# One attention and GLU decode step on one core: output weights loaded in sixteen pieces of eight partitions

## The chip, the cores and the metric

The kernel runs on one core of one Trainium2 chip. Time is device microseconds (us) of one execution, given as the median of several runs. The core has the engines TensorE (PE in the profile), VectorE (DVE), ScalarE (ACT), GpSimd (POOL) and SyncE (SP), and 16 DMA engines that move data between the chip's memory (HBM) and the on-chip memory (SBUF, 128 partitions). In this kernel SP issues every transfer, on one queue that each of the 16 DMA engines serves in order.

## The reference

The step takes `x` of 4 sequences, one token each, D = 512, and computes, in bf16:

```
h   = x + Attention(LayerNorm(x))
out = h + GLU(LayerNorm(h))

q = LN(x) @ wq                     # 32 heads of 128
p = softmax(q k^T / sqrt(128))     # k_cache, v_cache: [4, 32, 8192, 128]
Attention = (p v) @ wo             # wo: [4096, 512]
GLU = (sigmoid(LN(h) @ w_gate) * (LN(h) @ w_up)) @ w_down    # F = 1792
```

The two caches hold 128 pairs of sequence and head, and each pair has 2 MB of K and 2 MB of V: 537 MB that are read once. All weights together are 13.9 MB, of which `wo` is 4.2 MB.

## The kernel before

**Heads.** The 128 pairs ("heads" from here on, `NH`) are worked off one after another. A K head is transposed on TensorE (`transposes`, L360), copied from PSUM to SBUF by ScalarE and VectorE in turn (L370, L372) and multiplied with the query (`scores`, L385). Eight heads make a group, whose softmax is done at once. Nine heads later (`LAGH`) the V head is multiplied with the probabilities (`pv`, L469; L481 in the last group). After each group, `finish` and `project` bring the eight results through the output weights (L498) and add them to the residual. At the end come the second LayerNorm and the GLU (L593, L609).

**The ring.** K and V heads, and at the end the three GLU weights, go through a ring of eight slots of 2 MB (`NSL`, `KV`). `take_slot` hands the slots out in turn, and a load into a slot waits until TensorE has finished with the head that held it.

**The order of the loads.** All loads stand in one list, `order`: K head n at place 4n, V head n at place 4(n + 9), so ten K heads come first and then V and K in turn. `wq` is put behind K head 0. `pump` walks the list in the order of the program and emits a load on SP's queue as soon as the program knows what it must wait for; the chip keeps that order. A load that waits holds up all loads behind it.

**Output weights.** `wo` (4096 x 512) lies in `Wreg` as 128 partitions of 32 heads of 512 values: row 128 h + p of `wo` goes to partition p, place h. `Wreg` holds `wq` first, so every `wo` load waits for the end of the q projection (`t_qproj`, L533). Before the change there are four loads (L302), one behind each of K heads 2, 3, 4 and 5. Load i brings heads 8i to 8i + 7 of all 128 partitions: 1,024 rows of 1 KB, 1 MB. Each load has a semaphore of its own, and `project` waits for all four before its first matmul.

Of the kernel before, what the change touches and what calls it, by code (L numbers as in the profile page):

```python
# [13 lines left out]
NKT = 16  # L14
LAGH = 9
GH = 8


class _Prog:
# [27 lines left out]
    def emit(self, eng, fn, waits=(), incs=1):  # L47

        todo = self._waits(eng, waits)
        tok = self.token(eng, incs) if incs else None  # L50

        def run(e):
            for key, v in todo:
                e.wait_ge(self.sems[key], v)
            made = fn(e)
            made = made if isinstance(made, list) else [made]
            if incs:
                assert len(made) == incs
                for m in made:
                    m.then_inc(self.sems[eng], 1)  # L60

        self.ops[eng].append(run)
        return tok
# [14 lines left out]
def bass_sequential_preLN__mha_block_cached__glu_gated_glu__decode_kernel(  # L78
# [20 lines left out]
    NH = B * H  # L99
    NG = NH // GH  # L100
    SCALE = float(DH) ** -0.5
# [3 lines left out]
    prog = _Prog()  # L105
    emit = prog.emit

    with ExitStack() as es:
        def SB(name, shape, dt):
            return es.enter_context(nc.sbuf_tensor(name, shape, dt))  # L110

        ident = SB("ident", [128, 128], BF16)
        identf = SB("identf", [128, 128], FP32)
        M8 = SB("M8", [128, GH], FP32)
        Gmat = SB("Gmat", [128, 128], FP32)
# [10 lines left out]
        q_all = SB("q_all", [128, NH], BF16)  # L126
        Lq = SB("Lq", [128, 2, GH * W], BF16)
        KV = SB("KV", [128, NSL, R * 128], BF16)
        kTc = SB("kTc", [128, NKT, 512], BF16)
        S_sb = SB("S_sb", [128, 512], FP32)  # L130
        E_sb = SB("E_sb", [128, 512], BF16)
        PT = SB("PT", [128, 2, NK * GH * 32], BF16)
        mpart = SB("mpart", [128, 1], FP32)
        mrow = SB("mrow", [1, GH], FP32)
        negmb = SB("negmb", [128, 1], FP32)
        sig = SB("sig", [128, 1], FP32)
        rsum = SB("rsum", [128, 1], FP32)
        O_sb = SB("O_sb", [128, 512], FP32)
        OT = SB("OT", [128, 2, GH], BF16)
        sg_sb = SB("sg_sb", [128, NFT * B], FP32)  # L140
# [7 lines left out]
        wo_v = Wreg[:, :].rearrange("p (h f) -> p h f", h=H)  # L148
# [15 lines left out]

        keys = ["sp", "act", "dve", "pool", "pe", "x", "out", "wg", "wu", "wd0", "wd1"]
        keys += [f"sl{i}" for i in range(NSL)] + [f"k0p{i}" for i in range(4)] + [f"vl{i}" for i in range(4)]
        keys += [f"wq{i}" for i in range(4)] + [f"wo{i}" for i in range(4)]
        for k in keys:
            prog.sems[k] = es.enter_context(nc.semaphore("s_" + k))

# [17 lines left out]
        def cols(t, c):  # L188
            return t[:, c:c + NDC * (B - 1) + 1:NDC]
# [107 lines left out]
        t_wo = []  # L297
        t_qproj = []

        def emit_wo(i):  # L300
            src = A_wo.rearrange("(h p) f -> p h f", p=128)
            t_wo.append(prog.dma("sp", f"wo{i}", lambda e: e.dma_start(  # L302
                wo_v[:, 8 * i:8 * (i + 1), :], src[:, 8 * i:8 * (i + 1), :]), [t_qproj[0]]))

        order = []
        for n in range(NH):
# [2 lines left out]
        order.sort()  # L309
        order = [(k, n) for _, _, k, n in order]  # L310
        order.insert(1, ("wq", 0))
        for i, after in enumerate((2, 3, 4, 5)):
            order.insert(order.index(("k", after)) + 1, ("wo", i))
        order.insert(order.index(("v", NH - 3)), ("wg", 0))
        order += [("wu", 0), ("wd", 0)]
        t_w = {}
# [7 lines left out]
        def pump():  # L324
            while next_dma[0] < len(order) and ready(*order[next_dma[0]]):
                kind, n = order[next_dma[0]]
                next_dma[0] += 1
                if kind == "k":
                    emit_head("k", n, k_src(n), t_k, "k0p" if n == 0 else "")
                elif kind == "v":  # L330
                    emit_head("v", n, v_src(n), t_v, "vl" if n == NH - 1 else "")
                elif kind == "wq":
                    emit_wq()
                elif kind == "wo":
                    emit_wo(n)
                else:
                    emit_weight(kind)
# [152 lines left out]
        def project(g, t_ot):  # L490
            ob = g % 2

            def f(e):
                ins = None
                for c in range(NDC):
                    for hh in range(2):
                        h = 2 * g + hh
                        ins = e.matmul(cols(bank[XO][:, 64:64 + NDC * B], c), wo_v[:, h, 128 * c:128 * (c + 1)],  # L498
                                       OT[:, ob, B * hh:B * (hh + 1)], start=(hh == 0), stop=(hh == 1))
                return ins  # L500
            t = emit("pe", f, [t_ot, *t_wo])
            st_["ot"][ob] = t
            st_["h"] = st_["xo"] = emit("dve", lambda e: e.tensor_tensor(
                sth[:, 0:NDC * B], sth[:, 0:NDC * B], bank[XO][:, 64:64 + NDC * B], ALU.add), [t, st_["h"]])

        def finish(g):
            ob = g % 2
            t_oev[g] = emit("act", lambda e: e.activation(O_sb[:, :], bank[OBK], ACT.Copy),  # L508
                            [t_pvg[g], st_.get("sel")])
            box = {}  # L510

            def s1():
                def f(e):
                    ins = None
                    for q in range(4):
                        ins = e.matmul(bank[XO][:, 0:GH], O_sb[:, 128 * q:128 * (q + 1)],  # L516
                                       selq[:, q:q + 29:4], start=(q == 0), stop=(q == 3))
                    return ins
                t = emit("pe", f, [t_oev[g], t_sel, st_["xo"]])
                st_["sel"] = t  # L520
                box["ot"] = emit("dve", lambda e: e.tensor_copy(OT[:, ob, :], bank[XO][:, 0:GH]),  # L521
                                 [t, st_["ot"][ob]])

            def s2():
                project(g, box["ot"])
            return [(4, s1), (6, s2)]
# [22 lines left out]
        for u in range(4 * (NH + LAGH)):  # L549
# [20 lines left out]
            if vu >= 0:  # L570
                pv(vu // 4, vu % 4)
                if vu % 32 == 31 and vu // 32 < NG - 1:
# [8 lines left out]
        t_ot = emit("dve", lambda e: e.tensor_copy(OT[:, gl % 2, :], bank[OBK][:, 0:GH]),  # L581
                    [t_pvg[gl], st_["ot"][gl % 2]])
        project(gl, t_ot)
        t_hn, _ = layernorm(sth, st_["h"], 1, hnT, bank[XS], st_["xs"])

# [91 lines left out]
```

## Time and profile before

| | |
|---|---|
| median of 3 runs | 1316.87 us (1316.83 to 1317.15) |
| span of the profiled execution, first to last instruction | 1315.5 us |
| TensorE busy | 1016.4 us, 77% |
| VectorE busy | 721.1 us, 55% |
| ScalarE busy | 608.7 us, 46% |
| SP's DMA queue, share of the 16 DMA engines' time | 99.0% |
| bytes moved | 552.68 MB, mean 420 GB/s |
| a `wo` load of 1 MB, issue to landing (median) | 14.1 us |
| first matmul of `project` (L498) | 159.7 us |

The span covers one execution under the hardware profiler. It is 1.4 us shorter than the median of the timed runs, which also holds what lies before the first and after the last instruction. The slices of the page cut the span into 40 equal parts; a digit is the busy share in tenths, and GB/s is what all 16 DMA engines moved together. In the table of waits, "A <- B: us, times, longest" says for how long A stood still until B was done. Rows of the windows give, for each stretch, the busy time of PE, PEld (weight loads), DVE, ACT and POOL with the number of instructions, then the granted TensorE clock, the DMA share and GB/s. The trace also keeps a record of every DMA packet with its start, duration and size, and of every time at which a DMA engine counted a transfer's semaphore up.

### The profile page before, as it was taken

The page shows a single profiled execution, that of the slowest core. Times are in us where ns is not written, and L with a number is a line of the kernel's source. Part 1 is how long each engine was busy: PE and PEld are TensorE (multiplying, and loading weights), DVE is VectorE, ACT ScalarE, POOL GpSimd, SP SyncE. Part 2 cuts the span into 40 slices and gives each one's busy share as a digit, 9 for nine tenths or more (in the row PEclk, how much of TensorE's full clock was granted, in tenths as well). Part 3 has the DMA queues.
Part 4 walks back from the last instruction along what each step waited for, and adds up shares of the span by engine and source line. Part 5 has one row for each costly group of instructions (what it writes and reads, how often), then busy time and mean ns, then how long its engine had stood idle before and what let it go on. Part 6 is the DMA issues. An engine that isn't in the chain of part 4 may idle for free.

```text
span 1315.5 us, 29564 instructions
## 1 busy us (share of the span) xinstructions
PE 1016.4 (77%) x13385; PEld 671.9 (51%) x13385; DVE 721.1 (55%) x1210; ACT 608.7 (46%) x1095; POOL 9.0 (1%) x11
## 2 busy tenths in 40 slices
PE   6887877877788787887788778788887878778764
PEld 5654544545455454554455445455554545545443
DVE  5774655556555565555556456555555656556520
ACT  3664544545444454444445445454444545445420
POOL 2000000000000000000000000000000000000000
PEclk8988888888888888788888888888788888888865
DMA  9999999999999999999999999999999999999996
GB/s 381 415 427 426 427 427 427 425 428 425 428 425 426 427 425 428 424 427 426 427 426 426 426 428 424 427 425 428 427 424 426 426 428 425 426 427 428 425 411 245
DMA packets 45510, 552.68 MB, mean 420 GB/s; under 512 B 4420, under 2 KB 10312, under 8 KB 12360
## 3 DMA queue, kind: packets, MB, share of 16 engines
q1 hardware_dynamic: 45384, 550.79, 99.0%
q8 instruction: 105, 1.72, 0.5%
q14 instruction: 21, 0.17, 0.0%
HBM read 550.77 MB, written 0.00 MB: 419 GB/s over the span
## 4 chain that ended last, share of the span: by engine, by line
DMA 81%; PE 16%; SPq 2%; ACT 0%; issue 0%; DVE 0%
DMA KV<-in_A_v_cache_dram 76%; PE PS L360 10%; PE PS L385 3%; PE PS L469 3%; DMA KV<-in_B_w_down_dram 2%; DMA KV<-in_A_k_cache_dram 1%; SPq L277 1%; DMA Wreg<-in_A_wq_dram 1%; SPq L302 0%; SPq L295 0%; ACT kTc L370 0%; SPq L274 0%; ACT L422 0%; PE PS L533 0%; PE PS L481 0%
## 5 line engine op out<-in xcount | busy, mean ns | idle before, releaser
L372 DVE CAST kTc<-PS 128x512 bf16<-128x512 f32 x1024 | 676.1, 692 | 484.4 <-PE PS L360 481.6
L370 ACT ACTIVATE kTc<-PS 128x512 bf16<-128x512 f32 x1024 | 573.4, 595 | 648.2 <-PE PS L360 646.2
L360 PEld LDWEIGHTS PS<-ident,KV 128*128 128x128 bf16 x8192 | 547.5, 109 | 252.3 <-ACT kTc L370 135.7
L360 PE MATMUL PS<-ident,KV 128*128 128x128 bf16 x8192 | 654.7, 240 | 12.8 <-DMA KV<-in_A_k_cache_dram 10.4
L469 PE MATMUL PS<-KV,PT 128*32 128x512 bf16 x1920 | 216.8, 442 | 242.2 <-DMA KV<-in_A_v_cache_dram 242.2
L385 PE MATMUL PS<-kTc,Lq 128*32 128x512 bf16 x2048 | 227.1, 435 | 1.1 <-DVE Lq L545 0.6
L469 PEld LDWEIGHTS PS<-KV,PT 128*32 128x32 bf16 x1920 | 52.4, 99 | 273.9 <-DMA KV<-in_A_v_cache_dram 273.6
L385 PEld LDWEIGHTS PS<-kTc,Lq 128*32 128x32 bf16 x2048 | 53.5, 95 | 64.6 <-issue 19.1
L481 PE MATMUL PS<-PT,KV 128*128 128x1 bf16 x512 | 14.9, 165 | 18.0 <-DMA KV<-in_A_v_cache_dram 15.4
L481 PEld LDWEIGHTS PS<-PT,KV 128*128 128x128 bf16 x512 | 14.3, 104 | 18.6 <-DMA KV<-in_A_v_cache_dram 15.9
L516 PE MATMUL PS<-selq,O_sb 128*128 128x8 f32 x120 | 16.7, 266 | 7.1 <-ACT O_sb L508 7.1
L516 PEld LDWEIGHTS PS<-selq,O_sb 128*128 128x128 f32 x120 | 15.3, 200 | 10.0 <-ACT O_sb L508 10.0
L409 DVE TENSOR_REDUCE mrow<-PS 1x8 f32<-1x128 f32 x16 | 4.5, 279 | 29.2 <-PE PS L405 29.2
L205 ACT ACTIVATE lnw<-lnw 128x4 f32<-128x4 f32 x2 | 0.4, 205 | 38.9 <-DVE lnw L202 38.9
L581 DVE CAST OT<-PS 128x8 bf16<-128x8 f32 x1 | 0.2, 167 | 32.6 <-PE PS L481 32.6
L521 DVE CAST OT<-PS 128x8 bf16<-128x8 f32 x15 | 2.5, 167 | 19.5 <-PE PS L516 19.5
L422 ACT ACTIVATE E_sb<-S_sb,negmb 128x512 bf16<-128x512 f32 x16 | 11.6, 722 | 3.1 <-DVE negmb L420 2.6
L400 DVE TENSOR_REDUCE mpart<-S_sb 128x1 f32<-128x512 f32 x16 | 11.0, 686 | 3.1 <-ACT S_sb L398 1.5
L508 ACT ACTIVATE O_sb<-PS 128x512 f32<-128x512 f32 x15 | 9.0, 597 | 6.3 <-PE PS L469 6.3
L446 DVE CAST PT<-PS 128x512 bf16<-128x512 f32 x16 | 10.9, 682 | 0.7 <-PE PS L438 0.7
L398 ACT ACTIVATE S_sb<-PS 128x512 f32<-128x512 f32 x16 | 9.6, 597 | 1.2 <-PE PS L385 1.1
L405 PE MATMUL PS<-identf,mpart 128*1 128x128 f32 x32 | 7.5, 325 | 2.4 <-DVE mpart L400 2.4
(67 smaller groups left out, 119.5 us busy)
## 6 DMA issues: line engine op xcount, KB each, us to landing
KV<-in_A_k_cache_dram SPq DMA_DIRECT2D x127, 2048.0 KB, 28.7
KV<-in_A_v_cache_dram SPq DMA_DIRECT2D x127, 2048.0 KB, 33.1
Wreg<-in_A_wq_dram SPq DMA_DIRECT2D x4, 1024.0 KB, 11.7
Wreg<-in_A_wo_dram SPq DMA_DIRECT2D x4, 1024.0 KB, 14.1
KV<-in_A_k_cache_dram SPq DMA_DIRECT2D x4, 512.0 KB, 5.7
KV<-in_A_v_cache_dram SPq DMA_DIRECT2D x4, 512.0 KB, 26.6
KV<-in_B_w_gate_dram SPq DMA_DIRECT2D x1, 1792.0 KB, 28.1
KV<-in_B_w_up_dram SPq DMA_DIRECT2D x1, 1792.0 KB, 26.4
```

Source lines behind the costliest of these rows:

```text
L277: done[n] = [prog.dma("sp", f"sl{slot}", lambda e: e.dma_start(KV[:, slot, :], src), w)] * 4
L360: ins = e.matmul(bankT[g % NTB][:, 128 * i:128 * (i + 1)], KV[:, slot, r * 128:(r + 1) * 128], ident[:, :], start=True, stop=True)
L370: t_copy[g] = emit("act", lambda e: e.activation(kTc[:, ks, :], bankT[g % NTB][:, :], ACT.Copy), w)
L372: t_copy[g] = emit("dve", lambda e: e.tensor_copy(kTc[:, ks, :], bankT[g % NTB][:, :]), w)
L385: mms.append(e.matmul(PS[32 * j:32 * (j + 1), 512 * SBK:512 * (SBK + 1)], Lq[:, g % 2, off:off + 32], kTc[:, (n * NK + k) % NKT, :], start ...
L398: t_sev[g] = emit("act", lambda e: e.activation(S_sb[:, :], bank[SBK], ACT.Copy), [t_score[32 * g + 31], st_.get("exp")])
L400: t_mx = emit("dve", lambda e: e.tensor_reduce(mpart[:, :], S_sb[:, :], AX.X, ALU.max), [t_sev[g], st_.get("p1")])
L422: box["a2"] = emit("act", lambda e: e.activation(E_sb[:, :], S_sb[:, :], ACT.Exp, bias=negmb[:, 0:1], scale=SCALE, accum_out=sig[:, 0:1]), ...
L446: st_["xs"] = t_ptc[g] = emit("dve", lambda e: e.tensor_copy(dst, src), [t, t_pt0, t_pvg.get(g - 2)])
L469: mms.append(e.matmul(PS[32 * j:32 * (j + 1), 512 * OBK:512 * (OBK + 1)], PT[:, pb, o:o + 32], KV[:, slot, 512 * k:512 * (k + 1)], start=f ...
L481: ins = e.matmul(bank[OBK][:, i:i + 1], KV[:, slot, 128 * r:128 * (r + 1)], PT[:, pb, o:o + 1], start=(r == 0), stop=(r == R - 1))
L516: ins = e.matmul(bank[XO][:, 0:GH], O_sb[:, 128 * q:128 * (q + 1)], selq[:, q:q + 29:4], start=(q == 0), stop=(q == 3))
```

## The change

`wo` comes in sixteen loads of eight partitions each. Load i brings all 32 heads of partitions 8i to 8i + 7: 256 rows of 1 KB, 256 KB. The first stands behind K head 2, and each further one behind one more load of the ring, so the last stands between K head 13 and V head 4. All sixteen count one semaphore, and `project` waits for its final count (16 x 16). The bytes, their places in SBUF and the wait for the q projection are as before, and so is everything on the other engines.

```
+WOP = 8
...
-        keys += [f"wq{i}" for i in range(4)] + [f"wo{i}" for i in range(4)]
+        keys += [f"wq{i}" for i in range(4)] + ["wo"]
...
         def emit_wo(i):
             src = A_wo.rearrange("(h p) f -> p h f", p=128)
-            t_wo.append(prog.dma("sp", f"wo{i}", lambda e: e.dma_start(
-                wo_v[:, 8 * i:8 * (i + 1), :], src[:, 8 * i:8 * (i + 1), :]), [t_qproj[0]]))
+            t_wo.append(prog.dma("sp", "wo", lambda e: e.dma_start(
+                wo_v[WOP * i:WOP * (i + 1), :, :], src[WOP * i:WOP * (i + 1), :, :]), [t_qproj[0]]))
...
-        for i, after in enumerate((2, 3, 4, 5)):
-            order.insert(order.index(("k", after)) + 1, ("wo", i))
+        at = order.index(("k", 2)) + 1
+        for i in range(128 // WOP):
+            order.insert(at + 2 * i, ("wo", i))
...
-            t = emit("pe", f, [t_ot, *t_wo])
+            t = emit("pe", f, [t_ot, t_wo[-1]])
```

## The prediction

> **What bounds the kernel now.** I read the page from its slices inwards: first whether any engine or the transfers are busy all the way.
>
> ```profile
> PEclk8988888888888888788888888888788888888865
> DMA  9999999999999999999999999999999999999996
> GB/s 381 415 427 426 427 427 427 425 428 425 428 425 426 427 425 428 424 427 426 427 426 426 426 428 424 427 425 428 427 424 426 426 428 425 426 427 428 425 411 245
> DMA packets 45510, 552.68 MB, mean 420 GB/s; under 512 B 4420, under 2 KB 10312, under 8 KB 12360
> ...
> q1 hardware_dynamic: 45384, 550.79, 99.0%
> q8 instruction: 105, 1.72, 0.5%
> q14 instruction: 21, 0.17, 0.0%
> ```
>
> The transfers are busy in every slice at a flat 427 GB/s, 26.7 GB/s for each of the 16 engines; TensorE is at 77%. Only the last slice falls (6 tenths, 245 GB/s). So time is bytes on the busiest DMA engine. The chain of waits says the same:
>
> ```profile
> DMA 81%; PE 16%; SPq 2%; ACT 0%; issue 0%; DVE 0%
> DMA KV<-in_A_v_cache_dram 76%; PE PS L360 10%; PE PS L385 3%; PE PS L469 3%; DMA KV<-in_B_w_down_dram 2%; DMA KV<-in_A_k_cache_dram 1%; SPq L277 1%; DMA Wreg<-in_A_wq_dram 1%; SPq L302 0%; SPq L295 0%; ACT kTc L370 0%; SPq L274 0%; ACT L422 0%; PE PS L533 0%; PE PS L481 0%
> ```
>
> Third, the issues and their waits, to see how deep the queue is filled:
>
> ```profile
> KV<-in_A_k_cache_dram SPq DMA_DIRECT2D x127, 2048.0 KB, 28.7
> KV<-in_A_v_cache_dram SPq DMA_DIRECT2D x127, 2048.0 KB, 33.1
> ...
> Wreg<-in_A_wo_dram SPq DMA_DIRECT2D x4, 1024.0 KB, 14.1
> ...
> x_bf<-in_A_x_dram SPq DMA_DIRECT2D x1, 4.0 KB
> ```
>
> ```profile
> SPq L277 <- PE PS L385: 1114.4, 122, 13.2
> ...
> SPq L302 <- PE PS L533: 15.0, 1, 15.0
> ```
>
> A 2 MB load takes 4.9 us of the stream and lands 29 to 33 us after issue: six are queued at any time. SP waits 1114 us for free slots; issuing is not the limit. The x load has no landing time, and that is a clue used below. Last, the stretch in which the wo loads move, and the end:
>
> ```profile
> 24.00:42.00 18.00, 16.52 (x229) 12.51 (x230) 14.13 (x22) 12.13 (x23) 0.00 (x0) 0.88 1.02 412
> 42.00:60.00 18.00, 13.19 (x175) 9.69 (x172) 11.84 (x19) 9.95 (x18) 0.00 (x0) 0.91 1.04 418
> 60.00:96.00 36.00, 33.23 (x453) 23.46 (x454) 28.41 (x48) 24.70 (x45) 0.00 (x0) 0.91 1.01 427
> ...
> 1290.00:1312.00 22.00, 11.06 (x346) 10.31 (x347) 1.84 (x11) 1.71 (x3) 0.00 (x0) 0.50 0.61 231
> ```
>
> The last two columns are the DMA share and GB/s. With wo in the mix the rate is 412 to 418, and the share full: nothing idles there, so every added microsecond on the DMA engine that ends last moves the end. In the last 22 us the share is 0.61: some of the 16 engines have finished and others have not.
>
> **Two facts from the packet records behind these lines.** (1) A transfer does not always use 16 engines. Each engine ends its share with a 4-byte packet; there are 275 transfers of 16 such packets, and x, which has four partitions, has four data packets of 1 KB and four 4-byte packets. That is why its landing could not be computed. (2) The 16 engines do not keep step. The sixteen landings of one V load (last at 1298.4 us) lie, after the first, at 0.1, 0.3, 0.3, 0.7; 1.9, 5.9, 10.4; and eight between 18.5 and 20.7 us. At 53 us the spread was 2 us. The 105 instruction packets of 16 KB (q8) explain it: each stops one engine for about 1.05 us and stretches its next packet from 0.61 to 1.1, some 1.55 us; 13 on each of eight engines are 20 us. Five engines lead, three lie between, eight set the end.
>
> **The change, part by part.** *Rows.* wo remains 4 MB in 4,096 rows of 1 KB. Before, 128 partitions over 16 engines gave each engine 256 rows; the records have 46 ns for such a row (2 MB loads: 611 ns per 16 KB, 26.8 GB/s), so 11.8 us per engine. After, a load has eight partitions of 32 rows. By fact (1) I take it to run on eight engines, one partition each: 16 x 32 = 512 rows on the loaded engines, 23.6 us, and none on the others. Loaded: +11.8 us. Unloaded: -11.8 us.
>
> *Write rate into eight neighbouring partitions.* No row shows it for large loads. Lower end: no limit, 32 rows x 46 ns = 1.47 us per load, extra zero. Nearest row: the four x packets into four partitions took 44, 118, 47 and 44 ns, one slowed, though they hardly overlap. Upper end: in the 128-partition loads no eight partitions ever get more than one engine's rate; at that rate all 256 rows go through one lane, 11.8 us per load, 10.3 extra, 165 us in all. The rows speak for either end, so I take the geometric middle, 4.2 us per load (about three engines' worth): (4.2 - 1.47) x 16 = +43 us.
>
> [...]
>
> *Which engines.* If the loaded ones are among the leaders, part is absorbed. Chaining packets by their ends gives sixteen streams; the first four instruction packets (18.3, 29.2, 39.1, 49.1 us) each stop one of the four streams that began last on the first K piece (2.60 to 2.92 us; the first began at 2.15). If engines are started in number order, the eight late ones are the high half; I take the loaded eight as the low half. Their slowest is at 10.4 us against 20.7, a lead of 10.3 us. Other end: the late eight are loaded, lead 0.
>
> *Issue.* 16 issues in place of 4 on SP's queue: 12 x about 0.4 us = 5 us (rows of the SP timeline: 0.33 to 0.43 where the queue is not full). Hidden by the six loads queued ahead; were that cover gone, at most 5 us. Only the first wo load waits (15.0 us, for the q projection), as now, with the same K loads behind it. ACT's, POOL's, DVE's and PE's queues keep their instructions.
>
> *Landing.* The last wo load moves from behind K head 5 to between K head 13 and V head 4, whose issues now lie at about 88.5 us. The first reader, the projection at L498, starts at 159.7 us, after V head 7, queued three V and three K loads (29 us) behind. Cost zero; if that cover failed, the delay of one landing. The single semaphore is waited at 256, all loads: nothing is read early.
>
> *Order.* K heads 3 to 6 have less wo ahead of them (the last of them four loads of 256 KB in place of four of 1 MB), heads 7 to 13 more. Zero: the stream is full, so its length sets the end; if TensorE were short of K heads here, the few us of one of them.
>
> **Sum.** +11.8 + 43 - 10.3 = +45 us. The profiled span is 1315.5 us, and the median of the runs 1316.87, 1.4 more around it; I add to the median: **1362 us**.
>
> **Rivals.**
> (a) *No shared write limit.* For: the engines differ in phase by 2 us, longer than a 1.47 us share, so they may not meet; against: all eight reach each load within the same 2 us. Price: 11.8 - 10.3 = +1.5 us (1318.4) on leaders, +11.8 (1328.7) on late engines.
> (b) *One lane for all eight partitions.* +11.8 + 165 - 10.3 = +167 us, 1483. For: eight partitions are what one engine serves today. Against: eight engines pull at once.
> (c) *The split stays 16 ways.* 256 rows per engine as now: 1317. Against: the x load.
> (d) *Faster.* The late engines shed 11.8 us and the leaders absorb the rows. It decides where the added work falls under the 10.3 us lead: with rows at the 16 KB rate, 38.2 ns, 512 x 38.2 ns - 11.8 = 7.8 us, end -2.5 us, 1314.4; from 38 ns down it could be measured. Against: 46 ns was near constant over 4,096 rows.
>
> **How the numbers follow.** Forecast 0.62 (+20 to +76); (a) 0.21, of which leaders 0.13; (b) 0.08; (c) 0.04; (d) 0.05. A measurement here tells 0.2%, 2.6 us. Faster 0.05 from (d); same 0.12 from (c) and two thirds of (a) on leaders; slower 0.83. Range: low 1317 takes in (a); high 1393 is a middle of 5.4 us per load, when a lane also carries its own engine's K and V rows, without a lead: 11.8 + 63 = +75. The forecast's own range is 1337 to 1393.
>
> **What the next profile would show.** Right: 16 wo issues of 256 KB; 4-byte packets fewer by the 64 of four loads and more by 8 x 16; wo rows far above 46 ns (100 to 200); GB/s below 400 between about 25 and 130 us; then an average below 427 in no later slice by much; the last slice again only partly busy, with the other eight engines early. (a): rows at 46 ns and GB/s unchanged. (b): rows near 370 ns. (c): 16 small packets per wo load. Wrong would also be a wait of the projection at L498 for the weights, or SP short of slots so that the loaded engines run dry.

## The result and the profile after

The changed kernel takes 1385.32 us (median of 4 runs, 1382.65 to 1386.59) against 1316.85 us (4 runs, 1316.6 to 1317.15): 68.5 us more, a ratio of 1.0516 with a 95% interval of 1.0504 to 1.0529. The profiled execution has a span of 1380.9 us; the timed run of that same execution lies at 1382.65, 1.75 above it. The forecast was 1362 us, in a range of 1317 to 1393.

The slices of the changed kernel's page (40 slices of 34.5 us; granted TensorE clock, DMA share, GB/s, then packets and the share of SP's queue) show where the time went:

```profile
PEclk8877678888898889879888888988888888888865
DMA  9989999999999999999999999999999999999995
GB/s 342 276 234 245 252 382 426 426 428 425 426 427 426 427 426 426 427 426 427 427 425 427 427 426 427 427 426 425 427 428 425 424 428 426 424 427 422 425 417 222
DMA packets 45574, 552.68 MB, mean 400 GB/s; under 512 B 4484, under 2 KB 10376, under 8 KB 12424
...
q1 hardware_dynamic: 45448, 550.79, 98.3%
```

The DMA share stays at 9 tenths or just under in every slice but the last, but in slices 2 to 5 it moves only 234 to 276 GB/s. The engines are "busy" and slow: from 60 to 96 us the share is 0.94 at 242 GB/s (rows of the windows below), and a 16 KB packet under way with the rows of `wo` counts as busy for 937 ns on average, where it was 615 in the kernel before. From slice 7 on the rate is the old 427 and the end falls off as before. The stretches by window (PE, PEld, DVE, ACT, POOL, clock, DMA share, GB/s) place the loss more exactly:

```profile
24.00:60.00 36.00, 25.43 (x320) 18.95 (x320) 20.90 (x32) 17.90 (x32) 0.00 (x0) 0.81 1.04 282
60.00:96.00 36.00, 22.50 (x260) 16.61 (x260) 16.52 (x26) 14.47 (x26) 0.00 (x0) 0.81 0.94 242
96.00:132.00 36.00, 19.11 (x194) 12.52 (x190) 13.76 (x26) 11.88 (x21) 0.00 (x0) 0.69 0.89 250
132.00:168.00 36.00, 16.91 (x192) 10.95 (x188) 10.68 (x16) 9.12 (x16) 0.00 (x0) 0.69 0.95 249
168.00:204.00 36.00, 23.54 (x288) 15.27 (x288) 15.75 (x24) 13.46 (x24) 0.00 (x0) 0.77 1.00 357
204.00:240.00 36.00, 28.44 (x362) 18.65 (x366) 20.03 (x37) 17.40 (x32) 0.00 (x0) 0.86 1.01 427
```

Against 427 GB/s the five stretches from 24 to 204 us miss 145, 185, 177, 178 and 70 GB/s; times 36 us and divided by 427 that is 64 us of the stream, nearly all of the 68.5. The rows of `wo` were under way from 27.9 to 180.8 us in the packet records. What lies after runs as before, only later. The engines behind the transfers just wait: PE was busy for 22.5 us of the 36 us from 60 to 96, where it had been busy for 33.2.

The chain of waits keeps its shape, by engine and by line, with more of it under the transfers of K and V:

```profile
DMA 84%; PE 14%; SPq 2%; issue 0%; DVE 0%
DMA KV<-in_A_v_cache_dram 77%; PE PS L362 8%; DMA KV<-in_A_k_cache_dram 4%; PE PS L471 3%; PE PS L387 3%; SPq L278 2%; DMA KV<-in_B_w_down_dram 1%; DMA Wreg<-in_A_wq_dram 1%; SPq L296 0%; SPq L275 0%; SPq L303 0%; PE PS L483 0%; PE PS L535 0%; PE PS L611 0%; SPq L186 0%
```

The table of issues (engine, count, KB each, us from issue to landing) holds the first clue to the cause:

```profile
KV<-in_A_k_cache_dram SPq DMA_DIRECT2D x127, 2048.0 KB, 28.6
KV<-in_A_v_cache_dram SPq DMA_DIRECT2D x127, 2048.0 KB, 32.7
...
Wreg<-in_A_wo_dram SPq DMA_DIRECT2D x16, 256.0 KB
```

K and V heads land as fast as ever in the median, because most of them come after the bad stretch. `wo` has no landing time any more, just as the x load of four partitions had none before: its loads do not count their semaphore sixteen times. The packet records show how often: 4-byte completion packets went from 4,404 to 4,468, which is 64 fewer for four loads of 16 and 128 more for sixteen loads of 8. Each load runs on eight DMA engines.

SP's queue in order of time (start, duration, line, what) shows what that does to the loads behind:

```profile
26.46 0.34 SPq L303 DMA_DIRECT2D Wreg<-in_A_wo_dram  x1
26.84 9.30 SPq L278 DMA_DIRECT2D KV<-in_A_k_cache_dram  x1
36.18 0.34 SPq L303 DMA_DIRECT2D Wreg<-in_A_wo_dram  x1
36.56 9.22 SPq L278 DMA_DIRECT2D KV<-in_A_k_cache_dram  x1
...
155.49 0.64 SPq L303 DMA_DIRECT2D Wreg<-in_A_wo_dram  x1
156.17 9.25 SPq L278 DMA_DIRECT2D KV<-in_A_v_cache_dram  x1
...
193.21 0.33 SPq L278 DMA_DIRECT2D KV<-in_A_k_cache_dram  x1
```

Most `wo` issues take 0.34 us, and the K or V issue behind them about 9 us. I read this as a queue that is full on the slowest engines, so that nothing can be issued to the others either. The landings agree: of the K or V head whose last landing is at 112.2 us, eight engines landed within 0.2 us of each other and the other eight 9.2 to 15.2 us later. In the window from 96 to 132 us the DMA share is 0.89, so some engines had nothing to move. One pair of a `wo` load and a head passes every 10 us or so, where a head alone takes 4.9 us of the stream. Soon after the last `wo` load is out, an issue takes 0.33 us again.

The packet records give the price of a row. Before, the 4,096 rows of 1 KB took 46.1 ns on average. Now they take 94.5 ns (median 84, with 5% of them above 188). And the 16 KB packets of K and V in the same stretch are slower too: 937 ns on average, where they were 615. That second effect is the larger one. In the tables below, "K/V delay" is the sum of what 16 KB packets took above 613 ns while `wo` was loading, divided by 16 engines: 41.9 us here and 0.0 before.

### The profile page after: what moved, and what is told of

Read it like the earlier page. It is cut to its first block, busy times and chain, and to the rows that moved or that the text cites. A ratio compares the mean times of both kernels' runs of the same rounds, so it can differ in the third digit from the quotient of the medians.

```text
span 1380.9 us, 29575 instructions
## 1 busy us (share of the span) xinstructions
PE 1033.3 (75%) x13385; PEld 682.2 (49%) x13385; DVE 721.6 (52%) x1210; ACT 609.7 (44%) x1095; POOL 9.0 (1%) x11
## 4 chain that ended last, share of the span: by engine, by line
DMA 84%; PE 14%; SPq 2%; issue 0%; DVE 0%
DMA KV<-in_A_v_cache_dram 77%; PE PS L362 8%; DMA KV<-in_A_k_cache_dram 4%; PE PS L471 3%; PE PS L387 3%; SPq L278 2%; DMA KV<-in_B_w_down_dram 1%; DMA Wreg<-in_A_wq_dram 1%; SPq L296 0%; SPq L275 0%; SPq L303 0%; PE PS L483 0%; PE PS L535 0%; PE PS L611 0%; SPq L186 0%
## 5 line engine op out<-in xcount | busy, mean ns | idle before, releaser
L362 PEld LDWEIGHTS PS<-ident,KV 128*128 128x128 bf16 x8192 | 556.6, 110 | 286.7 <-ACT kTc L372 140.3
L362 PE MATMUL PS<-ident,KV 128*128 128x128 bf16 x8192 | 664.9, 243 | 43.1 <-DMA KV<-in_A_k_cache_dram 40.8
L471 PE MATMUL PS<-KV,PT 128*32 128x512 bf16 x1920 | 219.8, 448 | 260.4 <-DMA KV<-in_A_v_cache_dram 260.4
L387 PE MATMUL PS<-kTc,Lq 128*32 128x512 bf16 x2048 | 230.2, 441 | 1.1 <-DVE Lq L547 0.6
L483 PEld LDWEIGHTS PS<-PT,KV 128*128 128x128 bf16 x512 | 14.3, 104 | 17.9 <-DMA KV<-in_A_v_cache_dram 15.5
## 6 DMA issues: line engine op xcount, KB each, us to landing
Wreg<-in_A_wq_dram SPq DMA_DIRECT2D x4, 1024.0 KB, 11.8
KV<-in_B_w_gate_dram SPq DMA_DIRECT2D x1, 1792.0 KB, 27.8
```

Of the source, the lines that this page charges most:

```text
L362: ins = e.matmul(bankT[g % NTB][:, 128 * i:128 * (i + 1)], KV[:, slot, r * 128:(r + 1) * 128], ident[:, :], start=True, stop=True)
L387: mms.append(e.matmul(PS[32 * j:32 * (j + 1), 512 * SBK:512 * (SBK + 1)], Lq[:, g % 2, off:off + 32], kTc[:, (n * NK + k) % NKT, :], start ...
L471: mms.append(e.matmul(PS[32 * j:32 * (j + 1), 512 * OBK:512 * (OBK + 1)], PT[:, pb, o:o + 32], KV[:, slot, 512 * k:512 * (k + 1)], start=f ...
L483: ins = e.matmul(bank[OBK][:, i:i + 1], KV[:, slot, 128 * r:128 * (r + 1)], PT[:, pb, o:o + 1], start=(r == 0), stop=(r == R - 1))
```

## The experiments

The theory to test was an assumption of mine: that neighbouring partitions share a way into SBUF, called a lane here, that a lane carries no more than one DMA engine moves (26.7 GB/s on average in the kernel before), and so that eight engines writing eight neighbours hold up each other and the K and V packets that go the same way. No view shows a lane, nor which partitions would share one. What the runs can show is how the time of a row, of a K or V packet and of the kernel changes with the partitions of a load. The rivals: the uneven share of rows alone, the number and places of the small loads, or eight neighbouring rows read from one place in HBM. Every edit below is against the changed kernel, unless the text says otherwise, and each result is set against runs of the kernel before on the same chip (medians 1316.85 to 1317.06 us).

### Eight partitions four apart

```
-  wo_v[WOP * i:WOP * (i + 1), :, :], src[WOP * i:WOP * (i + 1), :, :]
+  wo_v[32 * (i // 4) + i % 4:32 * (i // 4 + 1):4, :, :],
+  src[32 * (i // 4) + i % 4:32 * (i // 4 + 1):4, :, :]
```

> The sixteen loads keep their size, number and places, but each brings eight partitions that lie four apart (32b + i, + 4, + 8 ... + 28) in place of eight neighbours. Lane theory (neighbouring partitions share a lane into SBUF that carries no more than one DMA engine's rate): the eight engines now write eight lanes, so most of the 68 us go; what stays is the uneven share of rows, 512 x 46 ns - 11.8 us = +11.8, less a lead of up to 10.3 us, plus what lanes lose that carry another engine's K and V rows as well: +2 to +19 us, rows near 46 ns. Rival 'share' (eight engines carry all rows, each row slow for a reason that has nothing to do with the partitions): +60 to +70 us as the changed kernel. Rival 'number' (sixteen small loads among the ring are what costs): +60 to +70 us.

1339.43 us, +22.5 (ratio 1.0174, 1.0159 to 1.0189). That is above the +2 to +19 that I gave for lanes, but two thirds of the loss are gone, with number, size and places of the loads as they were. So "number" falls, and so does a slow row that has nothing to do with its partition. The windows of this run:

```profile
24.00:60.00 36.00, 34.27 (x480) 25.57 (x480) 30.81 (x48) 26.27 (x48) 0.00 (x0) 0.92 1.01 413
60.00:96.00 36.00, 21.77 (x286) 14.68 (x286) 19.51 (x35) 17.02 (x30) 0.00 (x0) 0.89 1.00 341
96.00:132.00 36.00, 21.38 (x226) 13.49 (x227) 11.97 (x18) 10.31 (x18) 0.00 (x0) 0.69 0.93 310
132.00:168.00 36.00, 23.71 (x294) 15.47 (x293) 15.75 (x24) 13.68 (x25) 0.00 (x0) 0.78 1.00 412
168.00:204.00 36.00, 30.66 (x394) 20.03 (x393) 22.29 (x41) 19.13 (x35) 0.00 (x0) 0.88 1.01 427
```

The first 36 us, with loads into partitions 0 to 63, run at 413 GB/s, as fast as the kernel before in that stretch (412 to 418). The loss is between 60 and 132 us. The records split it the same way: the first half of the rows, partitions 0 to 63, took 46 ns, the second half, partitions 64 to 127, 61 ns, with a K/V delay of 12.9 us. Both halves came from the same eight engines: in the landings of every head from 54 to 144 us, eight engines finish within 2 us and the other eight follow at least 3 us behind, up to 9 us near 105 us, and this gap never closes, as it would if the upper half fell to the others. So it is where they write that differs. In this run the streams of the single engines can be told apart (a packet starts 3 to 4 ns before the last one of its engine ends): while the lower half loads, eight of the sixteen carry runs of 32 rows, and eight carry none.

### Sixteen loads of all partitions

```
-  wo_v[WOP * i:WOP * (i + 1), :, :], src[WOP * i:WOP * (i + 1), :, :]
+  wo_v[:, 2 * i:2 * (i + 1), :], src[:, 2 * i:2 * (i + 1), :]
```

> Sixteen loads of 256 KB in the same places, one semaphore, but each brings two heads of all 128 partitions, so all 16 engines carry 16 rows of each. Lane theory and 'share': no change against the kernel before, -3 to +3 us, rows at 46 ns. Rival 'number': most of the 68 us stay, since number, size and places of the loads are those of the changed kernel.

1316.57 us, -0.35 (ratio 0.9998, 0.9988 to 1.0007): no change. Rows take 46.4 ns, and neither GB/s nor the landing of `wo` (last figure, now there again) shows anything of the loads:

```profile
GB/s 382 423 423 427 427 426 428 426 427 424 428 425 427 426 427 428 426 427 426 427 426 427 427 426 427 427 427 426 426 427 427 426 427 427 426 428 426 426 409 253
...
Wreg<-in_A_wo_dram SPq DMA_DIRECT2D x16, 256.0 KB, 20.2
```

Twelve more issues on SP, 256 KB in place of 1 MB, the spread among the ring and the one semaphore cost nothing here. The whole loss comes with the narrow choice of partitions.

### Other rows of HBM, same partitions

```
-  wo_v[WOP * i:WOP * (i + 1), :, :], src[WOP * i:WOP * (i + 1), :, :]
+  wo_v[WOP * i:WOP * (i + 1), :, :], src[i:128:16, :, :]
```

> As the changed kernel in SBUF (eight neighbouring partitions in each load), but the eight rows read at a time lie 16 rows (16 KB) apart in HBM in place of side by side; the weights come to the wrong partitions, so the output is not the reference's, and the amount of work is the same. Lane theory: as slow as the changed kernel, +60 to +75 us. Rival 'source' (eight engines reading one 8 KB block of HBM at once is what is slow): +2 to +20 us.

1383.46 us, +66.5 (ratio 1.0514, 1.0466 to 1.0562), rows 91.3 ns, K/V delay 41.8 us: the changed kernel again. Whether the rows read at a time lie side by side in HBM or 16 KB apart makes no difference.

### Sixteen, 32 and 64 neighbours

```
-WOP = 8
+WOP = 16          # in the two others 32 and 64
-            order.insert(at + 2 * i, ("wo", i))
+            order.insert(at + 3 * i, ("wo", i))    # + 5 * i, + 9 * i
```

> Eight loads of sixteen neighbouring partitions (512 KB), each behind two more loads of the ring, over the same stretch of the list. Sixteen partitions should use all 16 engines, one partition each, so the rows are spread evenly: 256 per engine as before. 'Share': no change, -3 to +3 us. Lane theory: sixteen neighbours are served by lanes worth four engines (if eight are worth two, as the changed kernel's 94 ns per row and the slowed K and V rows suggest): 512 KB at 4 x 26.8 GB/s is 4.9 us per load, 39 us in place of 11.8, +27 to +35 us. If the lanes widen faster than that, less.

1363.5 us, +46.6 (ratio 1.0352, 1.0327 to 1.0378); rows 118.9 ns, K/V delay 27.8 us. Here `wo` has a landing time again, so all 16 engines take part and each carries 256 rows, as before the change; still it is slow. That ends the rival "share" for most of the loss. The size was more than the lane theory's 27 to 35, because that figure left out the K/V delay.

```profile
GB/s 332 287 286 296 330 427 426 427 425 428 425 427 427 426 426 427 426 426 427 427 426 428 425 428 425 426 428 427 425 426 427 426 427 426 426 421 418 427 415 237
...
Wreg<-in_A_wo_dram SPq DMA_DIRECT2D x8, 512.0 KB, 40.6
```

> Four loads of 32 neighbouring partitions (1 MB), spread over the same stretch; 16 engines with two partitions each, 256 rows per engine. Lane theory: more lanes, less loss. If the loss goes on falling by some 22 us with each doubling (68 at 8 partitions, 47 at 16): +20 to +28 us. [...] 'Share': 0.

> Two loads of 64 neighbouring partitions (2 MB), 16 engines with four partitions each. If the loss halves or more with each doubling of the partitions: 0 to +10 us. If 64 neighbours reach no more lanes than 32, it is as slow as the run with 32 partitions, within 5 us. 'Share': 0.

32 neighbours: 1343.85 us, +27.0 (ratio 1.0191, 1.016 to 1.0223), rows 96.8 ns, K/V delay 11.4 us. 64 neighbours: 1332.36 us, +15.5 (ratio 1.0119, 1.0104 to 1.0134), rows 88.9 ns, K/V delay 5.1 us. The row times are near each other and about twice 46; the times of the kernels are not within the 5 us that I had set for 64 neighbours that do no better than 32, since the K/V delay differs. The +27.0 lies inside the range for a loss that falls by some 22 us with each doubling; the +15.5 fits neither of its ranges. The GB/s of the 32 and then of the 64, whose two loads leave a pause between them:

```profile
GB/s 347 332 348 337 427 426 427 427 426 427 425 426 428 427 426 426 425 426 427 427 427 426 426 427 425 427 426 427 426 419 426 427 426 425 422 426 425 423 411 219
```

```profile
GB/s 345 366 324 426 424 430 424 427 427 425 427 427 425 428 425 427 427 424 429 425 426 427 426 428 426 425 429 426 426 426 425 428 426 425 426 427 427 427 409 250
```

### Eight partitions 16 apart, sixteen partitions 8 apart

```
-  wo_v[WOP * i:WOP * (i + 1), :, :], src[WOP * i:WOP * (i + 1), :, :]
+  wo_v[i:128:16, :, :], src[i:128:16, :, :]      # eight, 16 apart
   # and with WOP = 16, order.insert(at + 3 * i, ...):
+  wo_v[i:128:8, :, :], src[i:128:8, :, :]        # sixteen, 8 apart
```

> Sixteen loads of eight partitions that lie 16 apart (i, i + 16 ... i + 112), same places. Theory 'distance' (the farther apart the partitions, the less they get in each other's way): at most the +22.5 us of the run with partitions four apart. [...]

> [...] If only the number of partitions in a load counted: +46 us.

Eight partitions 16 apart: 1370.7 us, +53.6 (ratio 1.0399, 1.0367 to 1.0431), rows 75.3 ns, K/V delay 38.2 us. Four times as far apart as in the first experiment, and more than twice the loss: "distance" falls. Sixteen partitions 8 apart, in the places of the run with sixteen neighbours: 1348.03 us, +31.0 (ratio 1.0211, 1.0173 to 1.0249), rows 81.1 ns, K/V delay 22.2 us. That is 15.6 us better than sixteen neighbours (+46.6, 118.9 ns), so the number of partitions alone does not set the loss either. Both runs say that it depends on which partitions go together; neither says by what rule.

### The loads in the places of the kernel before

```
-            order.insert(at + 2 * i, ("wo", i))
+            order.insert(at + i + i // 4, ("wo", i))
```

> The changed kernel's sixteen loads of eight neighbours, but four at a time behind K heads 2 to 5, the places of the kernel before. If the places among the ring do not matter (lane theory: the rows and the traffic they meet are the same): +60 to +75 us. If mixing small loads with the ring's loads is what makes the lanes crowded: well under 50 us.

1369.12 us, +52.1 (ratio 1.0379, 1.034 to 1.0419). Neither expectation holds: with loads of eight neighbours the places do matter, by 16.4 us (52.1 against 68.5), but less than the partitions do. The rows themselves are slower (127.3 ns), and the K/V delay is smaller (21.8 us): beside the rows, 466 packets of 16 KB were moved in place of 2,072. I read this as row writers that meet more row writers, and fewer K and V packets, when four loads follow each other; no run tests it further.

### Who sets the end

The forecast took 10.3 us off, because the loaded engines were to be those that end early. Two runs leave out half of the weights.

```
   # half of the partitions: strides of the first experiment, and
-        for i in range(128 // WOP):
+        for i in range(64 // WOP):
   # control, against the kernel before: half of the heads, all partitions
-        for i, after in enumerate((2, 3, 4, 5)):
+        for i, after in enumerate((2, 3)):
```

> Left out: the output weights of partitions 64 to 127 (2 MB). The other 2 MB come as eight loads of eight partitions four apart, so eight engines carry 256 rows each, as many as in the kernel before, and the other eight none. Theory 'lead' (the eight engines that carry the rows are the ones that end about 10 us early; the eight without rows hold the instruction packets and set the end): the late eight shed 11.8 us and the end moves by the whole lead, -8 to -11 us. Rival 'late loaded' (the loaded eight are the late ones): 0, -2 to +1 us. If only bytes counted, 2 MB less over 16 engines: -5.9 us.

> Control for the run above. Left out: the output weights of heads 16 to 31 (the same 2 MB), by two loads of 128 partitions in place of four. Every engine sheds 128 rows of 46 ns: -5.9 us in all theories (-4 to -7).

The control is at 1311.66 us, -5.2 (ratio 0.9961, 0.9946 to 0.9975), near the -5.9 of its arithmetic. With the rows left out on eight engines alone, it is 1316.61 us, -0.2 (ratio 0.9998, 0.9988 to 1.0007): nothing. Rows are at 46.0 ns and the stream is hardly disturbed:

```profile
GB/s 383 400 419 427 426 427 426 427 425 427 426 427 425 426 428 426 426 427 426 428 426 425 426 427 425 427 421 428 424 428 426 427 427 423 427 425 425 428 409 214
...
Wreg<-in_A_wo_dram SPq DMA_DIRECT2D x8, 256.0 KB
```

Eight engines shed 11.8 us each, and the end did not move; so an engine that sets the end is among the loaded ones. The landings show which. Of the sixteen landings of one late V load, eight had been at 18.5 to 20.7 us after the first before the change. In this run six stand at 12.5 to 13.1 and two at 19.9 and 20.7. Six of the late eight were relieved, and two still carry rows. The six moved by 6 to 8 us, not by the 11.8 that they shed: in the head that ends at 80.6 us, the eight engines without rows are only 6 to 8 us ahead (0 to 0.5 us after the first landing, against 5.8 to 8.0). So the lead grew here by less than these engines were spared; I take the rest to be time in which these engines had nothing queued. The streams agree: of the first four instruction packets of this run (18.4, 29.2, 40.5, 48.6 us), the first three stop engines that carry no rows at the time, and the fourth stops one that does.

## Why the prediction was right or wrong

**What bounds the kernel** was right. Time is the stream on the engine that ends last: the slices, the windows and the chain of the changed kernel say the same, and 64 of 68.5 us are found as missing GB/s.

**Rows, +11.8 us.** Right. A load runs on eight engines (4,468 completion packets, no landing time, eight streams with runs of 32 rows), so 512 rows in place of 256 on the loaded ones.

**Write rate into eight neighbours, +43 us.** Right in kind, mis-sized: with 11.8 us for the rows and no lead, 68.5 - 11.8 = 56.7 us belong to it. I had counted only the rows: 4.2 us per load, 131 ns per row. The upper end of that middle, eight partitions that never take more than one engine's rate, was an assumption; no run came near the 370 ns per row that go with it (the slowest mean was 127.3). Rows alone took less, 94.5 ns, which is 512 x (94.5 - 46) = 24.8 us. The other 32 us go with the slower K and V packets (937 ns in place of 615); that they wait behind the rows on the same way into SBUF is my reading, and no run shows it. The forecast had them only at the upper end of its range (+75 without a lead). So it is partly luck that 43 came near 56.7: 18 us too much for the rows made up for more than half of the 32 us that were left out. How the K/V delay (41.9 us on average over 16 engines) splits between loaded and other engines isn't settled. Where all 16 engines carry the same rows, the two terms add up to the time without any such split: 256 rows above 11.8 us plus K/V delay gives 18.6 + 27.8 = 46.4 us for sixteen neighbours (measured 46.6), 13.0 + 11.4 = 24.4 for 32 (27.0), 11.0 + 5.1 = 16.1 for 64 (15.5) and 9.0 + 22.2 = 31.2 for sixteen partitions 8 apart (31.0). Where eight carry them, the sum is too large by 6 to 23 us; I take it that part of the delay falls on engines that had time to spare.

The runs side by side; rows, delay and time are measured, and the time is the change against the kernel before:

| partitions of a load | engines | mean ns per row | K/V delay, us | time, us |
|---|---|---|---|---|
| 128 | 16 | 46 | 0 | -0.35 |
| 8, four apart | 8 | 46 and 61 | 12.9 | +22.5 |
| 64 neighbours | 16 | 89 | 5.1 | +15.5 |
| 32 neighbours | 16 | 97 | 11.4 | +27.0 |
| 16, eight apart | 16 | 81 | 22.2 | +31.0 |
| 8, sixteen apart | 8 | 75 | 38.2 | +53.6 |
| 16 neighbours | 16 | 119 | 27.8 | +46.6 |
| 8 neighbours | 8 | 94 | 41.9 | +68.5 |
| 8 neighbours, packed | 8 | 127 | 21.8 | +52.1 |

Neither the number of partitions nor their distance alone orders these losses: eight partitions lost 22.5, 53.6 or 68.5 us and sixteen 31.0 or 46.6, and eight partitions 16 apart lost more than eight 4 apart.

**Which engines, -10.3 us.** Wrong, and this is the step that failed outright. Its reasoning was sound up to the last sentence: eight engines end late, instruction packets make them late. But I took four packets that stopped four late-starting streams for proof that all eight late engines were of the half without rows. By the landings six are, two are not, and one late engine among the loaded ones is enough. The half-load run shows a lead of zero. A lead counts by the slowest of the loaded engines, and the trace had shown me four of the eight. (The last landing of the V load that I read there lies at 1297.2 us in the records, not at 1298.4; its spread is as I gave it.)

**Issue, landing, order.** Issue and landing were right: sixteen loads of all partitions cost nothing, and the first projection (L500) starts at 224.5 us with no wait for weights, behind V heads that are themselves late. "Order: zero" held for loads of all 128 partitions (-0.35 us); with eight neighbours the places are worth 16.4 us.

**Rivals.** (a), no shared write limit, falls with rows at 94.5 ns. (b), one lane for all eight, would have needed rows near 370 ns. (c) falls with the count of completion packets. (d) would have needed the lead that wasn't there. Of the signs named beforehand, GB/s below 400 from 25 to 130 us came true and lasted about as long as the rows, to 181 us; rows of 100 to 200 ns were just missed by the mean.

## What to carry to other kernels

A load's share of the stream was here not only its bytes: the same 4 MB of `wo` cost 68.5 us more in loads of eight neighbours, on eight DMA engines, 46.6 more in loads of sixteen neighbours, on all 16, and nothing (-0.35 us) in sixteen loads of all 128 partitions. So count how many engines a load uses, and when the transfers set the time, try loads of all 128 partitions first. Small loads spread in a full queue cost nothing by themselves (the same -0.35 us); a narrow one also slowed the wide loads beside it, and here that cost more than its own rows (32 us against 24.8). When a lead among engines is to absorb something, ask for the slowest engine that gets the work, not for the typical one.

## What the runs showed of the hardware

- A high DMA share did not mean a high rate: in windows of 36 us the share stayed at 0.89 or above while the rate fell from 427 to 242 GB/s.
- Which partitions a load brings mattered more than how far apart they lie: eight partitions 4 apart cost 22.5 us, 16 apart 53.6 us, eight neighbours 68.5 us.
- A row of 1 KB took 46 ns in loads of all partitions and in the lower half of the loads four apart, and 61 in the upper half; 75 in loads of eight partitions 16 apart; 81 to 97 in loads of sixteen partitions 8 apart and of 64 and 32 neighbours; 94.5 and 119 in loads of eight and of sixteen neighbours; and 127 with the loads of eight neighbours packed.
- Narrow loads slowed the wide ones beside them: 16 KB packets of K and V took 937 ns on average beside loads of eight neighbours, and 615 beside the four loads of all partitions in the kernel before.
- Behind loads that use eight engines, K and V issues took 7.8 to 11.8 us (26 to 165 us), and 0.33 us from 175 us on, after the last such load; of the head that ends at 112.2 us eight engines finished within 0.2 us of each other and the other eight 9.2 to 15.2 us later, and the DMA share of that stretch fell to 0.89.
